# An attention, mixture-of-experts and gated FFN kernel: the parts of w_out made by the items of 512, w_in split in place, and groups that begin with the blocks still in SBUF

## The chip, the cores and the metric

The kernel runs on one core of one Trainium2 chip. The metric is the device time of one execution in microseconds (us). Before the change three runs took 1243.77 to 1248.26 us, median 1245.56. A separate, profiled execution took 1242.09 us, and its instructions span 1240.3 us; all durations in this document are from that execution.

The core has five engines with a queue each: TensorE (PE, matrix products; PEld are its weight loads), VectorE (DVE), ScalarE (ACT), GpSimd (POOL) and SyncE (SP, which here issues nearly all DMA requests).

## The reference, cut to what matters

Three stages follow one another: attention of 4096 rows against small states, a mixture of eight experts with one expert per token, and a gated FFN over 4608 tokens of width 512. The change touches the weights of the third stage, and the second stage only in that these weights are prepared beside it.

```python
# MoE: token t goes to one expert e
h = np.maximum(xc[mask] @ w1[e], 0.0)
y[mask] = gate_w[mask, None] * (h @ w2[e])
# FFN: w_in (512, 2048), w_out (2048, 512)
h = x @ w_in
relu6 = np.clip(h + 3.0, 0.0, 6.0)
g = h * relu6 / 6.0
return (g @ w_out).astype(np.float32)
```

## The kernel before, in words

**Number format.** The inputs are 64-bit floats. A float32 value is kept as two parts, hi (rounded to the shorter format `F32R` in which TensorE multiplies here) and lo (the rest), and a product is three matmuls: hi·hi, hi·lo, lo·hi (`PAIRS`). Making hi and lo is called a split: a copy on ScalarE (line 1239) and a subtraction on VectorE (line 1240).

**Stages.** Attention ends at about 130 us, with the routing of the tokens. The experts' tokens are then worked off in items of 512 (one written out in `first`, then a loop over `item_a`) until about 375 us, and in items of 128 (`item_b`) until about 449 us. The FFN takes the rest.

**Preparing w_in and w_out.** The 2048 hidden columns are 16 blocks f of 128. `Weights.load(f)` fetches a block's raw 64-bit w_in and w_out (512 KB each); `cut` makes float32 of them on VectorE with one step on ScalarE, four VectorE operations for each of the two; `keep` stores the float32 blocks (256 KB each) to a DRAM tensor `w32`. One block is cut during attention, three in the first item, and three in each round of the loop over `item_a`, at the places `LOAD_AT`, `CONV_AT` and `STORE_AT` of its eight steps. `again` fetches a block of `w32` back.

**FFN, first group.** 512 tokens (`first`) are multiplied plainly, block by block: `split_w(0, f)` and `split_w(1, f)` split the two weights into tiles W of [128, 2, 512], three buffers each; `stage_a(f)` makes h of the block in 12 matmuls (line 1308), applies the gate and splits g; `stage_b(f)`, two blocks later (`LAG`), adds the block's part of the output in 12 matmuls (line 1325). What is split is stored for the later groups: w_in's parts by `store_w`, four linear combinations of two blocks (made by `combine` from the float32 blocks, split, one pair p of blocks at a time) straight from a tile `both`, and w_out's parts by `store_o`. In DRAM, `wc` then holds 1792 KB for each of the eight pairs, and `wo` 1024 KB. In blocks 9, 11 and 13 `turn` also transposes and combines the x rows of the next group.

**FFN, groups of 768.** Five groups of 768 tokens use Strassen's scheme: `strassen(m)` computes seven products for one pair of blocks (line 1397), `second(m)` the output part (line 1449). Each of the 40 steps m reads back its pair of `wc` and `wo` (`load_c`, `load_o`), into two buffers each, two steps ahead; step m takes pair m mod 8.

**What sets the order.** The schedule is manual: each engine runs its instructions in the order in which the code is written, and waits at each for the data or buffers that it needs. SyncE's DMA requests are likewise in program order, so a request that waits holds those behind it. A request also waits until the eighth one before it, which had the same semaphore, has landed. The changed functions, with line numbers as in the profile:

## Time and profile before

| | |
|---|---|
| runs | 1243.77, 1245.56, 1248.26 us |
| profiled execution | 1242.09 us; span 1240.3 us |
| TensorE busy | 1160.9 us, 94% of the span |
| VectorE, ScalarE, GpSimd busy | 845.5, 503.0, 110.9 us |
| mean DMA rate | 221 GB/s, 273.68 MB in all |
| chain that ended last, by engine | PE 51%, DMA 6%, DVE 3%, ACT 2% |
| its largest lines | L1449 26%, L1397 23%, DMA `wc<-W` 4% |

A busy TensorE does not have to be at its peak: matmuls are pipelined, and the clock can be throttled to half. The granted clock is a share of full speed (2.4 GHz); a mean between 0.5 and 1 is a mix of the two levels. The chain of waits is followed back from the last instruction; a transfer in it, as `wc<-W`, is one for which an engine waited. A transfer is written destination<-source, by the names of tiles and DRAM tensors (`w` is `w32`; `cv`, `wf` and `W` are tiles in SBUF). In the lists of groups, `L1239` and `L1240` are the lines of the split helper and stand for many uses, which the tile names tell apart.

### The profile page before, as it was taken

How to read it: one execution, taken by the hardware profiler on the slowest of the kernel's cores; microseconds unless marked ns; L12 is line 12 of the kernel's file. 1: busy time of each engine (PE TensorE's matmuls, PEld its weight loads, DVE VectorE, ACT ScalarE, POOL GpSimd, SP SyncE). 2: the span in 40 equal slices, each digit the busy share in tenths (PEclk: the TensorE clock that was granted, in tenths of full speed). 3: DMA queues.
4: the chain of work that ended last, by engine and by line, in shares of the span. 5: the costliest groups of instructions: out<-in, count | busy, mean ns of one | idle time of the engine just before them, and what ended most of it. 6: DMA issues, size and time to landing. Idle time of an engine off the chain costs nothing.

```text
span 1240.3 us, 17749 instructions
## 1 busy us (share of the span) xinstructions
PE 1160.9 (94%) x6060; PEld 970.1 (78%) x6060; DVE 845.5 (68%) x1640; ACT 503.0 (41%) x955; POOL 110.9 (9%) x156
## 2 busy tenths in 40 slices
PE   7888999999998957778799999999999999999998
PEld 4665777888886635566699899889988999899997
DVE  6868787687681024456578876887688768876776
ACT  7776454354351123344243334333433343334331
POOL 4456301101101000000000000000000000000000
PEclk9889999999999978899999999999999999999999
DMA  6866887767666875666955565555655565456532
GB/s 191 269 220 204 295 263 254 235 222 254 241 216 231 298 273 180 249 227 233 368 200 198 204 229 213 203 191 212 218 196 202 203 238 186 173 187 238 185 144 85
DMA packets 103143, 273.68 MB, mean 221 GB/s; under 512 B 14240, under 2 KB 53152, under 8 KB 91040
## 3 DMA queue, kind: packets, MB, share of 16 engines
q1 hardware_dynamic: 98432, 261.20, 60.7%
q0 software_dynamic: 4640, 11.57, 2.6%
q8 instruction: 41, 0.67, 0.2%
q14 instruction: 30, 0.25, 0.1%
HBM read 208.47 MB, written 67.94 MB: 223 GB/s over the span
## 4 chain that ended last, share of the span: by engine, by line
PE 51%; DMA 6%; DVE 3%; ACT 2%; issue 1%; SPq 1%; ACTq 0%; DVEq 0%
PE o L1449 26%; PE b L1397 23%; DMA wc<-W 4%; DVE W L1240 1%; PE o L1235 1%; DMA wc<-wc 1%; ACT W L1239 1%; ACT both L1239 1%; PE b L1308 0%; DMA wo<-W 0%; DMA raw<-x_in_dram 0%; SPq L1178 0%; ACT g L1239 0%; SPq L1217 0%; DVE raw L1276 0%
## 5 line engine op out<-in xcount | busy, mean ns | idle before, releaser
L1449 PE MATMUL o<-wo,g 128*128 128x512 f32 x1440 | 334.3, 390 | 0.0
L1449 PEld LDWEIGHTS o<-wo,g 128*128 128x128 f32 x1440 | 269.7, 188 | 54.7
L1397 PE MATMUL b<-xc,wc 128*128 128x384 f32 x1680 | 301.2, 337 | 6.6 <-DMA wc<-wc 5.0
L1397 PEld LDWEIGHTS b<-xc,wc 128*128 128x128 f32 x1680 | 293.7, 189 | 9.3 <-issue 5.4
L1240 DVE TENSOR_TENSOR g<-cv,g 128x384 fp32r<-128x384 f32 x160 | 89.3, 558 | 92.8 <-ACT g L1239 92.8
L1239 ACT CAST g<-cv 128x384 fp32r<-128x384 f32 x160 | 82.2, 514 | 157.0 <-DVE cv L1251 157.0
L1458 DVE SCALAR_TENSOR_TENSOR W<-o,W 128x512 f32<-128x512 f32 x210 | 134.6, 681 | 3.5 <-PE o L1449 3.3
L872 PE MATMUL po<-w2p,hT 128*128 128x512 f32 x480 | 121.7, 401 | 0.0
L860 PE MATMUL ph<-xTa,w1p 128*128 128x512 f32 x480 | 117.4, 394 | 1.3 <-DVEq L1058 1.3
L1250 ACT ACTIVATE cv<-cv,three 128x384 f32<-128x384 f32 x80 | 49.3, 616 | 143.8 <-DVE cv L1411 136.3
L860 PEld LDWEIGHTS ph<-xTa,w1p 128*128 128x128 f32 x480 | 89.7, 188 | 22.8 <-issue 1.7
L872 PEld LDWEIGHTS po<-w2p,hT 128*128 128x128 f32 x480 | 89.9, 190 | 20.5 <-DVE hT L865 0.4
L1411 DVE TENSOR_TENSOR c<-b,c 128x384 f32<-128x384 f32 x160 | 87.0, 551 | 23.8 <-PE b L1397 23.2
L1308 PE MATMUL b<-xt,W 128*128 128x512 f32 x192 | 60.7, 472 | 26.1 <-ACT W L1239 25.4
L1308 PEld LDWEIGHTS b<-xt,W 128*128 128x128 f32 x192 | 43.4, 234 | 41.8 <-ACT W L1239 28.1
L1250 ACT ACTIVATE cv<-c,three 128x384 f32<-128x384 f32 x80 | 49.1, 614 | 15.0 <-DVE g L1240 15.0
L1411 DVE TENSOR_TENSOR cv<-b,cv 128x384 f32<-128x384 f32 x80 | 44.3, 554 | 14.3 <-PE b L1397 13.0
L1325 PE MATMUL o<-W,g 128*128 128x512 f32 x192 | 47.2, 393 | 2.9 <-ACT g L1239 2.9
L1251 DVE SCALAR_TENSOR_TENSOR cv<-cv,c 128x384 f32<-128x384 f32 x80 | 44.1, 552 | 5.8 <-ACT cv L1250 4.8
L277 PE MATMUL pxr<-BD,AT 128*128 128x265 f32 x128 | 42.2, 446 | 4.7 <-DVE AT L240 2.3
L775 DVE TENSOR_TENSOR w1p<-raw,w1p 128x512 fp32r<-128x512 f32 x48 | 31.9, 684 | 21.3 <-ACT w1p L774 16.6
L1325 PEld LDWEIGHTS o<-W,g 128*128 128x128 f32 x192 | 35.7, 188 | 12.1 <-ACT g L1239 3.7
(257 smaller groups left out, 1296.6 us busy)
## 6 DMA issues: line engine op xcount, KB each, us to landing
wc<-wc SPq DMA_DIRECT2D x40, 1792.0 KB, 7.1
raw<-in_moe_w_dram SPq DMA_DIRECT2D x80, 512.0 KB, 5.6
wo<-wo SPq DMA_DIRECT2D x40, 1024.0 KB, 6.0
raw<-in_moe_w_in_dram SPq DMA_DIRECT2D x16, 512.0 KB, 6.4
raw<-in_moe_w_out_dram SPq DMA_DIRECT2D x16, 512.0 KB, 5.0
x_in_dram<-XR SPq DMA_DIRECT2D x8, 1024.0 KB
w<-cv SPq DMA_DIRECT2D x32, 256.0 KB, 3.3
wc<-both SPq DMA_DIRECT2D x8, 1024.0 KB
```

What stands on the lines that cost most here:

```text
L860: nc.tensor.matmul(ph, lhsT=w1p[a][:, f, kk, :], rhs=xTa[b][:, kk, :], start=(n == 0), stop=(n == 11))
L872: nc.tensor.matmul(po[c], lhsT=hp[f][a][:, P * c:P * c + P], rhs=w2p[b][:, f, :], start=(f == 0 and n == 0), stop=(f == NF - 1 and n == 2),)
L1239: copy(hi, src)
L1240: nc.vector.tensor_tensor(lo, src, hi.bitcast(F32), op=ALU.subtract)
L1250: nc.scalar.activation(gg, h, AF.Relu, bias=k["three"])
L1251: nc.vector.scalar_tensor_tensor(gg, gg, 6.0, h, op0=ALU.min, op1=ALU.mult)
L1308: nc.tensor.matmul(ph, lhsT=W1[f][:, a, P * kk:P * kk + P], rhs=xt[b][:, kk, :], start=(n == 0), stop=(n == 11))
L1325: nc.tensor.matmul(pos[c], lhsT=gg[a][:, P * c:P * c + P], rhs=W2[f][:, b], start=(f == 0 and n == 0), stop=(f == NFF - 1 and n == 2),)
L1397: nc.tensor.matmul(t, lhsT=w[:, s:s + P], rhs=XC[m // NP][:, x, b, kk, :], start=(i == 0), stop=(i == 5))
L1411: v.tensor_tensor(c, t, u, op=ALU.add)
L1449: nc.tensor.matmul(po, lhsT=gs[f][a][:, o:o + P], rhs=w[:, DM * (2 * f + b):DM * (2 * f + b) + DM], start=(q == 0), stop=(q == 5),)
L1458: nc.vector.scalar_tensor_tensor(dst, po, 1.0 / 6.0, dst, op0=ALU.mult, op1=ALU.add)
```

## The change

- `cut` works on w_out first, then on w_in, and has a ninth step, `five`: it splits w_out's float32 block on ScalarE and VectorE into a tile `hl`. `keep` stores this pair of parts (512 KB) to `wo`, and w_in's float32 block (256 KB) to `w32`, now two tensors. `item_a` runs five steps instead of four in the second of each block's two places.
- The FFN no longer splits or stores w_out. It loads `wo` by pairs (`new_o`), two buffers, one pair ahead.
- w_in's parts and the combinations are written straight into one tile of 1792 KB per pair, in the layout of `wc` (two buffers of the pool that the groups use, and a third, `wcq`, for the pairs 2 and 5); `store(p)` stores it with one request. `stage_a` reads its weights there; the half of the odd block that the groups do not need is in a small tile `a21`.
- Each group of 768 starts with the two pairs that the stage before it ended with, which are still in SBUF; `pair_of` gives the order. Of 40 loads of each kind 30 are left in the groups.

```diff
--- before.py
+++ after.py
...
@@ -1001,7 +1001,7 @@
                     if f == CONV_AT[n]:
                         conv[n].begin()
                     if f in (CONV_AT[n], CONV_AT[n] + 1):
-                        conv[n].four()
+                        conv[n].some(4 + f - CONV_AT[n])
                 if f >= 1:
...
         self.raw = {}
 
         dram = tc.nc.dram_tensor
-        self.w32 = dram("w32", (NFF, 2, P, DM), F32, kind="Internal").ap()
+        self.w32 = dram("w32", (NFF, P, DM), F32, kind="Internal").ap()
+        self.wo = dram("wo", (NFF, P, 2 * DM), F32, kind="Internal").ap()
         self.wc = dram("wc", (NFF // 2, P, 7 * DM), F32, kind="Internal").ap()
-        self.wo = dram("wo", (NFF // 2, P, 4 * DM), F32, kind="Internal").ap()
 
...
-    def keep(self, f, a):
-
-        for i in range(2):
-            self.tc.nc.sync.dma_start(self.w32[ds(f, 1), i].rearrange("a p w -> p (a w)"), a[i])
-
-    def again(self, f, i, t=None):
-
-        t = self.room(i) if t is None else t
-        self.raw[f, i] = t
-        self.tc.nc.sync.dma_start(t, self.w32[f, i])
+            parts[i] = a[i]
+
+        def five():
+            t = parts[1] = self.two()
+            nc.scalar.copy(t[:, 0], a[1])
+            v.tensor_tensor(t[:, 1], a[1], t[:, 0].bitcast(F32), op=ALU.subtract)
+
+        return parts, [lambda g=g, i=i: g(i) for i in (1, 0) for g in (one, two, three, four)] + [five]
+
+    def keep(self, f, parts):
+
+        dma = self.tc.nc.sync.dma_start
+        dma(self.wo[ds(f, 1)].rearrange("a p w -> p (a w)"), parts[1].bitcast(F32).rearrange("p i w -> p (i w)"))
+        dma(self.w32[ds(f, 1)].rearrange("a p w -> p (a w)"), parts[0])
+
+    def again(self, f, t):
+
+        self.raw[f] = t
+        self.tc.nc.sync.dma_start(t, self.w32[f])
 
...
+    def load_w(f):
+        if f < NFF:
+            W.again(f, qp.tile([P, DM], F32, tag="wf", name="wf", bufs=4))
+
+    def new_c():
+        return sp.tile([P, 7 * DM], F32R, tag="wc", name="wc")
+
+    def new_o(p):
+        t = sp.tile([P, 4 * DM], F32R, tag="wo", name="wo")
+        nc.sync.dma_start(
+            t.bitcast(F32).rearrange("p (f w) -> p f w", f=2), W.wo[2 * p:2 * p + 2].rearrange("f p w -> p f w")
+        )
         return t
 
-    def split_w(i, f):
-        t = new_w(i, f)
-        split(t[:, 0], t[:, 1], W.raw[f, i])
+    def split_w(f):
+        p, odd = divmod(f, 2)
+        if not odd:
+            t = wc[p] = qp.tile([P, 7 * DM], F32R, name="wcq") if p % 3 == 2 else new_c()
+            split(t[:, 0:DM], t[:, DM:2 * DM], W.raw[f])
+        else:
+            a21[p] = qp.tile([P, 2, 2 * P], F32R, tag="a21", name="a21", bufs=2)
+            t = wc[p][:, 2 * DM:3 * DM].rearrange("p (i f) -> p i f", i=2)
+            for to, u in ((a21[p], 0), (t, 2 * P)):
+                split(to[:, 0], to[:, 1], W.raw[f][:, u:u + 2 * P])
 
     def combine(p):
 
-        a1, a2 = ([W.raw[2 * p + i, 0][:, 2 * P * u:2 * P * u + 2 * P] for u in range(2)] for i in range(2))
+        a1, a2 = ([W.raw[2 * p + i][:, 2 * P * u:2 * P * u + 2 * P] for u in range(2)] for i in range(2))
         t = W.scratch(1).bitcast(F32)
         s = [t[:, 2 * P * i:2 * P * i + 2 * P] for i in range(4)]
...
-        nc.sync.dma_start(W.wc[p, :, 3 * DM:].rearrange("p (i f) -> p i f", i=2), both.bitcast(F32))
-
-    def store_w(f):
-        p, o = divmod(f, 2)
-        if o == 0:
...
+    def store(p):
+        nc.sync.dma_start(W.wc[p], wc[p].bitcast(F32))
+
+    def w1(f, a, kk):
+        p, odd = divmod(f, 2)
+        if odd and kk < 2:
+            return a21[p][:, a, P * kk:P * kk + P]
+        o = 2 * DM + 2 * P * a + P * (kk - 2) if odd else DM * a + P * kk
+        return wc[p][:, o:o + P]
 
...
@@ -1368,17 +1389,27 @@
         return rest
 
 
-    wc, wo = {}, {}
+    pair_of, pos_of = [], list(range(NP - 2, NP)) + list(range(NP - 2))
+    for n in range(len(groups)):
+        pair_of += pos_of
+        pos_of = pos_of[-2:] + pos_of[:-2]
+    cm, om = {}, {}
 
     def load_c(m):
-        if m < NP * len(groups):
-            wc[m] = sp.tile([P, 7 * DM], F32R, tag="wc", name="wc")
-            nc.sync.dma_start(wc[m].bitcast(F32), W.wc[m % NP])
+        if m < total:
+            p = pair_of[m]
+            if m < 2:
+                cm[m] = wc[p]
+            elif m % NP < 2:
+                cm[m] = cm[m - 2]
+            else:
+                cm[m] = new_c()
+                nc.sync.dma_start(cm[m].bitcast(F32), W.wc[p])
 
     def load_o(m):
-        if m < NP * len(groups):
-            wo[m] = sp.tile([P, 4 * DM], F32R, tag="wo", name="wo")
-            nc.sync.dma_start(wo[m].bitcast(F32), W.wo[m % NP])
+        if m < total:
+            p = pair_of[m]
+            om[m] = wo[p] if m < 2 else om[m - 2] if m % NP < 2 else new_o(p)
 
 
...
@@ -1474,19 +1505,19 @@
             fetch(pairs.pop(0))
 
 
+    for p in range(2):
+        wo[p] = new_o(p)
+    load_w(2)
+    load_w(3)
     fetch(32, True)
     fetch(0, True)
     for f in range(2):
-        split_w(0, f)
-    load_w(0, 2)
-    load_w(0, 3)
-    split_w(1, 0)
+        split_w(f)
     combine(0)
     todo = []
     for c, (c0, h) in enumerate(first):
         pt = transposed(out_bank(), xw[c0][:, h])
         split(xt[0][:, :, P * c:P * c + P], xt[1][:, :, P * c:P * c + P], pt)
-    load_w(1, 2)
     fetch_next()
     fetch_next()
     new_xc(0, cp)
@@ -1494,33 +1525,31 @@
     LAG = 2
     for f in range(NFF + LAG):
         if f < NFF:
+            load_w(f + 4)
+            if f % 2 == 0:
+                store(f // 2)
             stage_a(f)
             if f + 2 < NFF:
-                load_w(0, f + 4)
-                split_w(0, f + 2)
+                split_w(f + 2)
                 if f % 2:
                     combine((f + 2) // 2)
-            if f + 1 < NFF:
-                split_w(1, f + 1)
-                load_w(1, f + 3)
         if f >= LAG:
             stage_b(f - LAG)
-        if f < NFF:
-            store_w(f)
-            store_o(f)
+            if f % 2 and f // 2 + 1 < NP:
+                wo[f // 2 + 1] = new_o(f // 2 + 1)
         for low in todo:
             low()
         todo = []
         if f in turns:
             todo.append(turn(0, turns[f], [bank(2), bank(3)]))
             fetch_next()
-        if f >= NFF - 2:
-            load_c(f - NFF + 2) if f < NFF else load_o(f - NFF)
+    for m in range(2):
+        load_c(m)
+        load_o(m)
     out_first()
     q0.close()
     cp1 = ctx.enter_context(tc.tile_pool(name="f_c1", bufs=1))
     turns = {1: 0, 3: 1, 5: 2}
-    total = NP * len(groups)
     for m in range(total + 1):
         n, p = divmod(m, NP)
```

**Order, SyncE, where the FFN begins.** These are the first requests after the loop of the items of 128, before the change. `raw` is the tile of x rows, `wf` and `cv` hold float32 blocks of w_in and w_out; the waits in brackets are semaphores, DMAHW0 to 7 those of the earlier requests.

```order
L1217 DMA raw_3002<-x_in_dram 32x512 [waits DMASW5_49,DMASW4_49,DMAHW4_49,DMASW3_49,DMASW2_49]
L1217 DMA raw_3002<-x_in_dram 32x512 [waits DMAHW5_49]
L1217 DMA raw_3002<-x_in_dram 32x512 [waits DMAHW6_49]
L1217 DMA raw_3002<-x_in_dram 32x512 [waits DMAHW7_49]
L1217 DMA raw_3002<-x_in_dram 32x512 [waits DMAHW0_49]
```

And after it, at the same place, where `wo` is the pair tile of w_out's parts:

```order
L1286 DMA wo<-wo 128x2x1024 [waits DMAHW2_49,DMASW5_49,DMAHW4_49,DMASW4_49,DMAHW5_49,DMASW3_49,DMAHW6_49,DMASW2_49,DMAHW7_49,Activation_49,Pool_49]
L1286 DMA wo<-wo 128x2x1024
L1189 DMA wf<-w 128x512 x2
L1228 DMA raw_3027<-x_in_dram 32x512 x2
L1228 DMA raw_3027<-x_in_dram 32x512 [waits DMAHW0_49]
L1228 DMA raw_3027<-x_in_dram 32x512 [waits DMAHW1_49]
L1228 DMA raw_3027<-x_in_dram 32x512 [waits DMAHW2_49]
L1228 DMA raw_3027<-x_in_dram 32x512 [waits DMAHW3_49]
L1228 DMA raw_3027<-x_in_dram 32x512 [waits DMAHW4_49]
L1228 DMA raw_3027<-x_in_dram 32x512 [waits DMAHW5_49]
```

Two pairs of `wo` and two blocks of w_in now stand ahead of the x rows, and the fifth to eighth x request waits for the semaphores of just these four.

**Order, SyncE, one pair of blocks in the first group.** Before, for one even and one odd block (`both` are the combinations, `W` the split weights, `128x2x256` the odd block's half):

```order
L1178 DMA wf<-w 128x512
L1279 DMA wc<-both 128x2048
L1178 DMA cv_3140<-w 128x512
L1286 DMA wc<-W_3017 128x2x256
L1292 DMA wo<-W_3096 128x1024
L1178 DMA wf<-w 128x512
L1178 DMA cv_3172<-w 128x512
L1284 DMA wc<-W_3093 128x1024
L1292 DMA wo<-W_3137 128x1024
```

After, two pairs:

```order
L1315 DMA wc<-wc 128x3584
L1189 DMA wf<-w 128x512
L1286 DMA wo<-wo 128x2x1024
L1189 DMA wf<-w 128x512
L1315 DMA wc<-wcq 128x3584
L1189 DMA wf<-w 128x512
L1286 DMA wo<-wo 128x2x1024
L1189 DMA wf<-w 128x512
```

Nine requests per pair, five of them stores, have become four, one of them a store.

**Order, VectorE, in an item of 512.** Before, from one block's second conversion to the next step's ReLU part (`hT`), w_out's float32 block is `cv_2583`:

```order
L1161 SCALAR_TENSOR_TENSOR cv_2583<-raw_2485,cv_2583 128x512
L1165 ISA
L1165 SCALAR_TENSOR_TENSOR cv_2583<-raw_2485,cv_2583 128x512
L775 REGISTER_ALU
L775 TENSOR_TENSOR w1p_1858<-raw_0_96,w1p_1857 128x512
```

And after, where this place works on w_in (`cv_2595`) and then subtracts for w_out's parts (`hl`):

```order
L1165 SCALAR_TENSOR_TENSOR cv_2595<-raw_2496,cv_2595 128x512
L1169 ISA
L1169 SCALAR_TENSOR_TENSOR cv_2595<-raw_2496,cv_2595 128x512
L1176 REGISTER_ALU
L1176 TENSOR_TENSOR hl<-cv_2557,hl 128x512
L775 REGISTER_ALU
L775 TENSOR_TENSOR w1p_1861<-raw_0_96,w1p_1860 128x512
```

One subtraction has come in ahead of the item's own split of its expert weights (`w1p`).

## Rows read from the trace of the kernel before

**Rows 1.** Table by stage: microseconds, busy time (instructions) of each engine, clock, DMA
```profile
130.00:184.00 54.00, 51.07 (x251) 41.27 (x250) 44.65 (x117) 24.96 (x48) 11.08 (x11) 0.97 0.83 284
285.00:335.00 50.00, 50.00 (x226) 40.60 (x225) 36.79 (x62) 22.37 (x41) 8.07 (x12) 1.00 0.72 241
449.00:459.30 10.30, 3.91 (x17) 3.17 (x17) 6.69 (x12) 5.05 (x8) 0.00 (x0) 0.50 0.70 230
513.00:531.00 18.00, 13.76 (x53) 10.59 (x51) 8.59 (x14) 6.52 (x11) 0.00 (x0) 0.91 0.60 220
585.00:600.00 15.00, 7.18 (x27) 4.46 (x26) 7.19 (x12) 4.49 (x7) 0.00 (x0) 1.00 1.02 364
600.00:615.00 15.00, 13.41 (x68) 13.09 (x68) 8.02 (x16) 5.08 (x10) 0.00 (x0) 0.89 1.03 392
754.00:1219.80 465.80, 465.80 (x2372) 421.32 (x2371) 352.65 (x661) 171.77 (x320) 0.00 (x0) 1.00 0.55 197
```

**Rows 2.** Chain of waits: start, length (us), what held it, in the first group
```profile
459.29 5.04 PE b L1308 x12
...
487.69 3.82 DMA wc<-W
...
497.75 4.85 DMA wc<-W
...
504.96 3.88 DMA wc<-W
```

**Rows 3.** Groups by form, 459.3 to 585: count, busy us, mean ns, idle before, releasers
```profile
L1308 PE MATMUL b<-xt,W 128*128 128x512 f32 x192 | 60.7, 472 | 26.1 <-ACT W L1239 25.4 <-issue 0.7
...
L1250 ACT ACTIVATE gg<-b,three 128x512 f32<-128x512 f32 x15 | 10.3, 685 | 5.2 <-PE b L1308 5.2
L1240 DVE TENSOR_TENSOR g<-gg,g 128x512 fp32r<-128x512 f32 x14 | 9.7, 692 | 9.6 <-ACT g L1239 9.6
...
L1240 DVE TENSOR_TENSOR W<-cv,W 128x512 fp32r<-128x512 f32 x14 | 9.6, 683 | 0.0
L1251 DVE SCALAR_TENSOR_TENSOR gg<-gg,b 128x512 f32<-128x512 f32 x14 | 9.5, 679 | 5.2 <-ACT gg L1250 5.2
L1239 ACT CAST g<-gg 128x512 fp32r<-128x512 f32 x14 | 8.7, 620 | 17.7 <-DVE gg L1251 17.7
...
L1240 DVE TENSOR_TENSOR both<-raw,both 128x1024 fp32r<-128x1024 f32 x7 | 8.6, 1225 | 7.8 <-ACT both L1239 7.8
L1239 ACT CAST both<-raw 128x1024 fp32r<-128x1024 f32 x7 | 7.4, 1051 | 15.6 <-DVE raw L1276 15.6
L1235 PE MATMUL b<-ident,raw 128*128 128x128 f32 x24 | 3.1, 272 | 0.0
L1276 DVE TENSOR_TENSOR raw<-wf,raw 128x256 f32<-128x256 f32 x7 | 3.0, 425 | 0.2
```

**Rows 4.** Timeline where the first group of 768 begins
```profile
599.76 13.24 PE L1397 MATMUL b<-xc,wc 128*128 128x384 f32 x66 [4.96 <-DMA wc<-wc]
```

**Rows 5.** Timeline inside an item of 512, TensorE
```profile
242.15 2.94 PE L860 MATMUL ph<-xTa,w1p 128*128 128x512 f32 x12
...
247.72 2.94 PE L860 MATMUL ph<-xTa,w1p 128*128 128x512 f32 x12
```

**Rows 6.** DMA issues, whole kernel: size of each, median us to landing
```profile
wc<-wc SPq DMA_DIRECT2D x40, 1792.0 KB, 7.1
...
wo<-wo SPq DMA_DIRECT2D x40, 1024.0 KB, 6.0
...
cv<-w SPq DMA_DIRECT2D x18, 256.0 KB, 3.7
...
wf<-w SPq DMA_DIRECT2D x14, 256.0 KB, 5.0
...
wc<-W SPq DMA_DIRECT2D x8, 256.0 KB, 7.6
```

**Rows 7.** SyncE's own waits, whole kernel: us in total, times, longest
```profile
SPq L1172 <- DMA w<-cv: 53.2, 12, 5.6
```

More of the change, by code (lines that the diff above doesn't have):

```diff
@@ L969, in begin, with some @@
                 c.a, c.steps = self.W.cut(c.raw)
-            def four(c):
-                for step in c.steps[:4]:
+            def some(c, n):
+                for step in c.steps[:n]:
                     step()
-                del c.steps[:4]
+                del c.steps[:n]
             def store(c):
@@ L1061, in run @@
         for f in range(2):
-            for i in range(2):
-                self.W.again(f, i)
+            self.W.again(f, self.W.room(0))
         turned32(xb[:, 0:DM], x32)
@@ L1125, in room, with two @@
         return self.rp.tile([P, DM], F32, tag=f"cv{i}", name=f"cv{i}", bufs=2)
+    def two(self):
+        return self.rp.tile([P, 2, DM], F32R, tag="hl", name="hl", bufs=3)
     def load(self, f):
@@ L1143, in cut @@
         a, m = [None, None], [None, None]
+        parts = [None, None]
         words = [r.rearrange("p (f w) -> p f w", w=2) for r in raw]
@@ L1165, in four @@
             v.scalar_tensor_tensor(a[i], m[i], least, a[i], op0=ALU.is_ge, op1=ALU.mult)
-        return a, [lambda g=g, i=i: g(i) for i in range(2) for g in (one, two, three, four)]
-    def keep(self, f, a):
-        for i in range(2):
-            self.tc.nc.sync.dma_start(self.w32[ds(f, 1), i].rearrange("a p w -> p (a w)"), a[i])
-    def again(self, f, i, t=None):
-        t = self.room(i) if t is None else t
-        self.raw[f, i] = t
-        self.tc.nc.sync.dma_start(t, self.w32[f, i])
+            parts[i] = a[i]
[11 more added lines that the diff above has]
+        self.tc.nc.sync.dma_start(t, self.w32[f])
 def ffn(tc, ctx, W, x_in, out, k):
@@ L1254, in halves @@
         return [t[:, i] for i in range(2)]
-    W1, W2 = {}, {}
-    def new_w(i, f):
-        (W1, W2)[i][f] = t = sp.tile([P, 2, DM], F32R, tag=f"W{i}", name=f"W{i}", bufs=3)
-        return t
-    def split_w(i, f):
-        t = new_w(i, f)
-        split(t[:, 0], t[:, 1], W.raw[f, i])
+    wc, wo, a21 = {}, {}, {}
+    total = NP * len(groups)
+    first = [(32, 0), (32, 1), (0, 0), (0, 1)]
+    q0 = ExitStack()
+    qp = q0.enter_context(tc.tile_pool(name="f_q", bufs=1))
+    xt = [qp.tile([P, 4, 512], F32R, name=f"xt{i}") for i in range(2)]
+    def load_w(f):
[8 more added lines that the diff above has]
+        )
+        return t
+    def split_w(f):
[8 more added lines that the diff above has]
+                split(to[:, 0], to[:, 1], W.raw[f][:, u:u + 2 * P])
     def combine(p):
-        a1, a2 = ([W.raw[2 * p + i, 0][:, 2 * P * u:2 * P * u + 2 * P] for u in range(2)] for i in range(2))
+        a1, a2 = ([W.raw[2 * p + i][:, 2 * P * u:2 * P * u + 2 * P] for u in range(2)] for i in range(2))
         t = W.scratch(1).bitcast(F32)
@@ L1276, in combine @@
         v.tensor_tensor(s[3], a1[1], s[1], op=ALU.subtract)
[L1277 to L1301 removed]
+        split(wc[p][:, 3 * DM:5 * DM], wc[p][:, 5 * DM:], t)
+    def store(p):
[6 more added lines that the diff above has]
+        return wc[p][:, o:o + P]
     def stage_a(f):
@@ L1308, in stage_a @@
                 nc.tensor.matmul(
-                    ph, lhsT=W1[f][:, a, P * kk:P * kk + P], rhs=xt[b][:, kk, :], start=(n == 0), stop=(n == 11)
+                    ph, lhsT=w1(f, a, kk), rhs=xt[b][:, kk, :], start=(n == 0), stop=(n == 11)
                 )
                 n += 1
-        gg = qp.tile([P, 512], F32, tag="gg", name="gg")
+        gg = W.room(1)
         gate(ph, gg)
@@ L1325, in stage_b @@
                 nc.tensor.matmul(
-                    pos[c], lhsT=gg[a][:, P * c:P * c + P], rhs=W2[f][:, b], start=(f == 0 and n == 0),
+                    pos[c], lhsT=gg[a][:, P * c:P * c + P], rhs=wo[f // 2][:, DM * (f % 2 * 2 + b):][:, 0:DM], start=(f == 0 and n == 0),
                     stop=(f == NFF - 1 and n == 2),
@@ L1332, in out_first @@
             c0 = first[2 * u][0]
-            oc = new_w(u, "out").bitcast(F32)
+            oc = W.two().bitcast(F32)
             nc.scalar.mul(oc[:, 0], pos[2 * u], 1.0 / 6.0)
@@ L1438, in second @@
         gs = [g.pop((m, i)) for i in range(2)]
-        w = wo.pop(m)
+        w = om[m]
         for c in range(6):
@@ L1442, in second @@
             if p == 0 and h == 0:
-                acc[i] = new_w(n % 2, ("out", n, i)).bitcast(F32)
+                acc[i] = W.two().bitcast(F32)
             po = out_bank()
@@ L1610, in begin @@
                 todo.extend(steps + [lambda: W.keep(f, a)])
-            return [begin] + [lambda: todo.pop(0)() for _ in range(9)]
+            return [begin] + [lambda: todo.pop(0)() for _ in range(10)]
         todo = []
```

19 lines of the change are left out of this document (1 added, 18 removed).

## The prediction

> **What bounds the kernel now.** I read the table by stage first [rows 1]. From 754 to 1219.8 us TensorE is busy 465.80 of 465.80 at a granted clock of 1.00: the groups of 768 tokens are TensorE's, and fewer loads there buy nothing. The items of 512 (285 to 335) are the same: TensorE 50.00 of 50.00, VectorE 36.79, ScalarE 22.37. The exception is the FFN's first group, about 459 to 600: in 513 to 531 TensorE is busy 13.76 of 18 us at clock 0.91, VectorE 8.59, ScalarE 6.52, DMA share 0.60. Nothing is full there, so something goes round in a circle.
>
> The chain of waits [rows 2] shows it: "DMA wc<-W" returns at every block, and from 487.69 to 504.96, one pair of blocks, takes 17.27 us. A tile of W is made, stored, and made again only when its store three blocks earlier has landed; SyncE's queue, nine requests per pair, holds the next store behind the combinations. The table by form [rows 3] agrees: TensorE's `stage_a` matmuls sat idle 26.1 us, 25.4 for ScalarE's W. At the end [rows 4] TensorE waits 4.96 us more, until 599.76, for `wc` to be read back.
>
> How much of this is needed? In the items one block of 24 such matmuls goes from 242.15 to 247.72 [rows 5]: 5.57 us, 0.232 us each. The group has 16 blocks: 89.1 us, where the trace has 459.29 to 594.80 (599.76 less the 4.96) = 135.5.
>
> **The first group after the change.** Removed: 16 splits of w_out (one 0.62 us copy on ScalarE and one 0.683 us subtraction on VectorE each [rows 3]), the 16 stores of 512 KB behind them, the store-before-reuse circle of W, the four read-backs (2 x 1792 and 2 x 1024 KB) at the end. Added: eight loads of 1024 KB of `wo`. The w_in parts are made in place, in three pair tiles in turn, and each pair is one store of 1792 KB, issued about four blocks before its tile is reused: about 22 us for something that lands in 7 when read [rows 6].
>
> *Start.* SyncE leaves the loop at the same moment, but puts 2 x 1024 KB of `wo` and 2 x 256 KB of w_in ahead of the x rows that `stage_a` needs, and four of the last six x requests also wait for those to land. A 256 KB request stuck behind others shows what a queue costs: the `wc<-W` stores of 256 KB land in 7.6 us, loads of 256 KB into `cv` in 3.7 [rows 6]. 2.62 MB at the 392 GB/s of 600 to 615 [rows 1] is 6.7 us. Bounds: 0 if the x rows pass the others, 22 if the four land one after another (6.0 + 6.0 + 5.0 + 5.0 [rows 6]). I take 6.7, nearest to the rate row: first `stage_a` matmul at 459.29 + 6.7 = 466.0.
>
> The Trainium skill, page "DMA: Bandwidth & Descriptors", section "Queues, rings and completion order", says that each DMA engine consumes a queue's descriptors in ring order. The 7.6 against 3.7 agrees with it. By that rule the sum carries the whole 6.7; without it the start would not move and the forecast would be 6.7 lower.
>
> *Length.* Matmuls 89.1; the 24 transposes of the three turns 3.1 [rows 3]; the first twelve matmuls at half clock (5.04 [rows 2] instead of 12 x 0.232 = 2.8) 2.3; a gap of 0.6 before the third block, whose split follows the first block's gate. Beside this run ScalarE and VectorE, now with less to do. Their chain per pair, by durations of [rows 3]: even block: ReLU 0.685, times h 0.679, cast 0.62, subtraction 0.692, split of w_in 0.683 = 3.4. Odd block: the same 2.7 to the gate's end, two half-width subtractions 0.8, four combinations of 0.425 = 1.7, cast 1.051, subtraction 1.225 = 7.4. Together 10.8 against TensorE's 11.1: covered, since `stage_b` lags two blocks, but just. A pair with a turn adds five half-width operations and two subtractions on VectorE (5 x 0.42 + 0.69 + 1.22 = 4.0) and 1.0 on TensorE: 14.8 against 12.2, so up to 2.6 shows per such pair; the lag absorbs part; I take 1.2 each, 3.6. Sum 98.7 (bounds 95.1 without turns' excess, 112 with it in full and the clock below). End at 564.7.
>
> Transfers as cover: per pair 1.84 MB stored, 1.05 + 0.52 loaded, 3.4 MB, which at 364 GB/s (585 to 600 [rows 1]) is 9.4 us of 11.1. So TensorE is next, with ScalarE/VectorE and DMA both within two microseconds of it.
>
> *Clock.* Granted clock is 0.50 (1.2 GHz) in 449 to 459.3 after the wait for the last scatter, 0.91 in the holed stretch, 1.00 where TensorE never stops [rows 1]. I assume 1.00 after the first block. The skill's page "TensorE: Matmul & The Clock Gate", section "HAM oscillation", says that idle gaps between bursts send the array back to half rate. The rows agree in direction. If gaps remain and 0.91 stays, 92.2 us of TensorE work takes 101: 9 more.
>
> *Into the groups.* The blocks of the first two steps are in SBUF, so the 4.96 us wait goes; that is part of the difference of the ends, 599.76 - 564.7 = 35.1. From there to the steady state ScalarE and VectorE pace both kernels (13.41 of 15 TensorE at 0.89 in 600 to 615 [rows 1]); I leave it at 0. The ten pairs of loads saved later lie under a full TensorE: 0.
>
> **What moves into the items.** 16 copies and 16 subtractions, the same forms. Twelve come in the loop: 3 x 0.683 more on VectorE per item, 36.79 to 38.8 of 50, 22.37 to 24.2 on ScalarE. TensorE covers that unless a block is locally full: between 0 and 12 x 0.683 = 8.2; I take 0.5. The stores grow by 256 KB each, but the second of the two no longer waits for the first (now different tensors; SyncE waited 53.2 us in 12 such waits [rows 7]), so what is queued behind it, the next loads, starts earlier; nothing on TensorE waits for these, so no gain. Three come in the first item (130 to 184), where VectorE is busy 44.65 of 54 and TensorE already waits 2.9 us: 0 to 2.1, I take 1.5. One falls to the attention: 0 to 0.7, I take 0.5. Together 2.5 (0 to 11).
>
> **Sum.** Profiled execution 1242.09 (span 1240.3 and 1.8 around it) - 35.1 + 2.5 = 1209.5. The median shown, 1245.56, lies 3.5 above that execution; half of this goes on top: 1211. Its own range, from the bounds that I think likely together (start 4 to 10, length 96 to 104, items 0 to 6): 1203 to 1221.
>
> **Rivals.**
> *Transfers pace the group.* For: DMA runs at 220 GB/s today in this stretch with a share of only 0.6 [rows 1], so latency may be what limits it, and store, load and x rows share one queue. 8 x 3.4 MB less the first two `wo` loads is 25.1 MB, at 220 GB/s 114 us: end at 580, gain 19.8, time 1227. Against: buffers are two to four deep and 364 to 392 GB/s are shown at the end of this same stage. 18%.
> *The items pay in full.* VectorE is locally full in blocks with a conversion (2.5 us of conversion, 0.68 more, three more of about 0.69, of 5.57): all 11 appear, 1220. Against: 13 us of slack per item. 6%.
> *The change doesn't overlap what it says:* `stage_a` waits for each gate-and-split chain and each chain for `stage_a`: 2 x 2.8 + 10.8 = 16.4 per pair, 131 in all, end at 597: time 1244 against 1245.56, no change. Against: order and lag above. 4%.
> *The round trip gets longer (slower).* SyncE still waits at each 1792 KB store for that pair's last subtraction, and loads are queued behind it. If load, split, combination, store and the next `wo` load then follow one another, a pair takes 5.0 + 7.5 + 7.1 + 6.0 = 25.6 us, 205 in all, time about 1318. It decides once a pair takes more than about 16.4 us, (599.76 - 466.0 - 2.5) / 8. Against: w_in is loaded four blocks ahead. 4%.
>
> **How the numbers follow.** Forecast 68%, then 18, 6, 4 and 4. The range 1197 to 1233 holds the forecast's own range, the items' case and the transfers' case, and below 1203 a start that does not move. About 0.3% (4 us) is what a measurement of this kernel can tell from no change. Faster 0.92, same 0.04, slower 0.04.
>
> **What would show it.** In the profile after: first `stage_a` matmul near 466 plus the items' 2.5; `stage_a` without idle time for ScalarE's cast; about 5.6 us per block; first matmul of the first group of 768 near 567, with no "DMA wc" before it; the items' slices unchanged on TensorE; DMA near 300 GB/s in the first group; from there to the end the same 640 us. Wrong if: blocks take 7 us or more with "DMA wo" or "DMA wf" as releaser (transfers); TensorE waits in the items for VectorE's hT or po; x rows land later than 10 us after the loop's end.

## The result, and the profile after

The changed kernel takes 1203.53 us (median of 4 runs, 1201.31 to 1206.39), the kernel before, run beside it, 1246.2 us: a ratio of 0.966, 95% interval 0.963 to 0.969. The profiled execution took 1204.09 us; its span fell from 1240.3 to 1202.3, by 38.0.

The table by stage for the kernel after, with the columns of [rows 1] (length; busy time and instructions of TensorE, its weight loads, VectorE, ScalarE, GpSimd; granted clock; DMA share; GB/s). Its stages are: an item of 512, the gap between the items and the FFN, the part of the first group that holds most of the turns' work, the begin of the groups of 768, and the long middle of the groups.

```profile
285.00:335.00 50.00, 50.00 (x226) 40.61 (x225) 38.43 (x63) 24.26 (x44) 8.82 (x14) 1.00 0.78 256
450.00:466.60 16.60, 3.65 (x16) 3.27 (x16) 6.11 (x12) 4.62 (x8) 0.00 (x0) 0.50 0.74 243
...
523.00:553.00 30.00, 30.00 (x142) 24.98 (x141) 23.73 (x46) 16.25 (x30) 0.00 (x0) 1.00 0.70 266
...
563.00:578.00 15.00, 13.40 (x78) 13.04 (x77) 9.79 (x19) 5.27 (x11) 0.00 (x0) 1.00 0.58 193
718.00:1183.80 465.80, 465.80 (x2368) 420.84 (x2367) 352.95 (x662) 171.05 (x317) 0.00 (x0) 1.00 0.44 159
```

In the item TensorE still has no free moment while VectorE went from 36.79 to 38.43 us. In the first group, where TensorE had been busy 13.76 of 18 us, it is now busy 30.00 of 30. In the groups the DMA share fell from 0.55 to 0.44 and 465.80 us of TensorE stayed 465.80.

The chain of waits of the kernel after (start, length, what held it) where [rows 2] had "DMA wc<-W" at every block:

```profile
451.85 7.13 DMA wf<-w
459.00 3.04 DMA raw<-x_in_dram
462.29 3.65 PE o L1246 x16
...
466.65 5.52 PE b L1329 x12
...
478.19 2.72 PE o L1346 x12
480.91 2.72 PE b L1329 x12
```

Blocks now follow one another at 2 x 2.72 us, and the wait for W's stores is gone. New at the top is a wait for W_in ahead of the x rows. The groups by form of the same stretch, 466.6 to 563.1, answer to [rows 3]: TensorE's idle time before `stage_a` was 26.1 us, and is 0.8 + 0.0 + 1.3.

```profile
L1346 PE MATMUL o<-wo,g 128*128 128x512 f32 x192 | 47.0, 392 | 0.7 <-ACT g L1250 0.7
...
L1329 PE MATMUL b<-xt,wc 128*128 128x512 f32 x108 | 29.6, 420 | 0.8 <-issue 0.7
...
L1329 PE MATMUL b<-xt,a 128*128 128x512 f32 x48 | 12.2, 389 | 0.0
...
L1329 PE MATMUL b<-xt,wcq 128*128 128x512 f32 x36 | 9.2, 396 | 1.3 <-DVE wcq L1251 1.3
```

And the timeline where the first group of 768 begins, answering to [rows 4], has no wait in brackets:

```profile
563.08 11.63 PE L1428 MATMUL b<-xc,wc 128*128 128x384 f32 x66
```

With four moments read off the timelines of every run (first matmul of the items; SyncE's first request of the FFN, "exit"; first `stage_a` matmul; first Strassen matmul), the span divides as follows, in us. The names are those of the experiments below.

| kernel | first item to exit | exit to stage_a | stage_a to Strassen | Strassen to end | span |
|---|---|---|---|---|---|
| before | 316.1 | 10.4 | 140.5 | 640.5 | 1240.3 |
| after | 317.7 | 15.7 | 96.4 | 639.2 | 1202.3 |
| e1 reload | 318.7 | 15.9 | 97.2 | 639.1 | 1202.8 |
| e2 x first | 318.7 | 10.5 | 96.6 | 639.3 | 1197.8 |
| e3 w_out in the FFN | 319.2 | 14.1 | 101.8 | 639.2 | 1205.8 |
| e4 deep (before) | 315.1 | 10.5 | 104.5 | 641.4 | 1205.0 |
| e5 five twice | 332.9 | 15.6 | 91.0 | 639.2 | 1202.1 |
| e6 two stores | 319.3 | 15.6 | 92.0 | 639.3 | 1189.8 |
| e8 two tiles | 318.9 | 16.1 | 91.1 | 639.2 | 1191.0 |
| e9 early store (before) | 317.9 | 10.5 | 105.2 | 641.0 | 1199.4 |
| e10 after again | 319.2 | 15.8 | 94.1 | 639.2 | 1199.2 |
| e11 x first, two tiles | 317.9 | 10.1 | 92.4 | 639.3 | 1189.6 |
| e7 x first, turns | 320.4 | 10.4 | 93.0 | 639.2 | 1195.6 |

The whole gain is in the third column. What precedes the first item varies from set to set with the same code (131 to 134 us in before, after and e1 to e4, 123 to 126 in e5 to e9, 130 to 133 in e10, e11 and e7), and the kernel before had medians of 1246.0, 1238.4 and 1243.1 beside these sets. So times are compared as ratios to the kernel before of the same set, spans only by columns.

### The profile page after: what moved, and what is told of

It reads as the page before. It is cut to its first block, busy times and chain, and to the rows that moved or that the text cites. A ratio compares the mean times of both kernels' runs of the same rounds, so it can differ in the third digit from the quotient of the medians.

```text
span 1202.3 us, 17646 instructions
## 1 busy us (share of the span) xinstructions
PE 1146.1 (95%) x6060; PEld 962.2 (80%) x6060; DVE 845.6 (70%) x1648; ACT 502.9 (42%) x963; POOL 110.4 (9%) x156
## 2 busy tenths in 40 slices
DMA packets 98342, 244.84 MB, mean 204 GB/s; under 512 B 13280, under 2 KB 50144, under 8 KB 92640
## 4 chain that ended last, share of the span: by engine, by line
PE 56%; DVE 3%; DMA 1%; ACT 1%; issue 1%; SPq 0%; DVEq 0%; ACTq 0%
PE o L1480 27%; PE b L1428 24%; PE b L1329 2%; PE o L1346 1%; PE o L1246 1%; ACT g L1250 1%; DVE cv L1262 1%; DMA wf<-w 1%; DVE wc L1251 1%; DMA wc<-wc 1%; ACT wc L1250 0%; DVE xc L1388 0%; DMA raw<-x_in_dram 0%; DVE g L1251 0%; DVE xc L1387 0%
## 5 line engine op out<-in xcount | busy, mean ns | idle before, releaser
L1480 PE MATMUL o<-wo,g 128*128 128x512 f32 x1440 | 334.3, 390 | 0.0
L1480 PEld LDWEIGHTS o<-wo,g 128*128 128x128 f32 x1440 | 269.7, 188 | 54.7
L1251 DVE TENSOR_TENSOR g<-cv,g 128x384 fp32r<-128x384 f32 (+1 forms) x176 | 100.4, 571 | 103.8 <-ACT g L1250 103.8
L1250 ACT CAST g<-cv 128x384 fp32r<-128x384 f32 (+1 forms) x176 | 92.1, 523 | 181.6 <-DVE cv L1262 181.6
L1489 DVE SCALAR_TENSOR_TENSOR hl<-o,hl 128x512 f32<-128x512 f32 x210 | 134.7, 682 | 3.5 <-PE o L1480 3.3
L1346 PE MATMUL o<-wo,g 128*128 128x512 f32 x192 | 47.0, 392 | 0.7 <-ACT g L1250 0.7
L1262 DVE SCALAR_TENSOR_TENSOR cv<-cv,cv 128x384 f32<-128x384 f32 x80 | 43.9, 549 | 0.0
L1346 PEld LDWEIGHTS o<-wo,g 128*128 128x128 f32 x192 | 35.7, 188 | 9.7 <-ACT g L1250 1.5
L1452 ACT COPY c<-b 128x384 f32<-128x384 f32 x40 | 19.2, 480 | 55.1 <-PE b L1428 54.9
L1164 ACT ACTIVATE raw<-raw 128x512 f32<-128x512 f32 x32 | 22.1, 690 | 46.2 <-DVE cv L1160 46.0
```

The lines of the kernel that those rows point to most:

```text
L1250: copy(hi, src)
L1251: nc.vector.tensor_tensor(lo, src, hi.bitcast(F32), op=ALU.subtract)
L1262: nc.vector.scalar_tensor_tensor(gg, gg, 6.0, h, op0=ALU.min, op1=ALU.mult)
L1346: nc.tensor.matmul(pos[c], lhsT=gg[a][:, P * c:P * c + P], rhs=wo[f // 2][:, DM * (f % 2 * 2 + b):][:, 0:DM], start=(f == 0 and n == 0), s ...
L1480: nc.tensor.matmul(po, lhsT=gs[f][a][:, o:o + P], rhs=w[:, DM * (2 * f + b):DM * (2 * f + b) + DM], start=(q == 0), stop=(q == 5),)
L1489: nc.vector.scalar_tensor_tensor(dst, po, 1.0 / 6.0, dst, op0=ALU.mult, op1=ALU.add)
```

## The experiments

**What paid: the circle.** e4 is the kernel before with one edit, the tiles of W_in four deep instead of three; w_out, the separate pair tiles and all loads stay as they were.

```
-  ... tag=f"W{i}", name=f"W{i}", bufs=3)
+  ... tag=f"W{i}", name=f"W{i}", bufs=4 - i)
```

> The kernel before, with the w_in tiles W four deep instead of three (more does not fit beside its other tiles). Nothing else is changed: the same stores, loads, splits and queue. Theory A1 (the circle split, store, reuse holds the first group): a split may now wait for a store one block older, the 40.5 us that ScalarE waits for DMA wc<-W mostly go, and a pair falls from 17.3 us to what ScalarE and VectorE or the queue need, 13.5 to 15: 18 to 30 us less, 1216 to 1228. Theory A3 (SyncE's queue itself, nine requests per pair in order, each waiting for the combinations or for the eighth request before it, is what holds): less than 5 us, 1241 or more.

Measured: 1208.26 us, 0.970 (0.967 to 0.973). The idle time of ScalarE before its copy into a W_in tile, by form, first in the kernel before (459 to 600), then in e4 (459 to 585):

```profile
L1239 ACT CAST W<-wf 128x512 fp32r<-128x512 f32 x14 | 8.7, 619 | 40.5 <-DMA wc<-W 40.5
```
```profile
L1239 ACT CAST W<-wf 128x512 fp32r<-128x512 f32 x14 | 8.6, 618 | 2.7 <-DMA wc<-W 2.7
```

One more buffer gives 35.3 of the 38.0 us of span, more than the 18 to 30 us of A1, whose mechanism it shows; A3 falls. Is it memory, then, that the kernel before lacked? e9 goes back to three tiles and only issues each store one block earlier.

```
+    store_w(0)
     for f in range(NFF + LAG):
...
-            store_w(f)
+            if f + 1 < NFF:
+                store_w(f + 1)
```

> Tests the circle in the kernel before without giving it a byte more of SBUF. The kernel before with its three tiles of W_in, in which the store of a tile is issued one block earlier: that of tile 0 ahead of the loop, that of tile f+1 at the end of block f. Theory A (the store was issued so late that its landing fell into the time in which the tile was wanted again): the wait of ScalarE for W's stores, 40.5 us in the kernel before, falls below 10 us and the time comes to that of the kernel before with four tiles, 1206 to 1212. Theory B (three tiles are too few, whenever the store is issued): the wait stays above 25 us and the time above 1230.

Measured: 1201.12 us, 0.9685 (0.9636 to 0.9735), which is 1207 us at the 1246 us that the kernel before took in the first set: theory A, with not a byte more. By form, ScalarE's same row and TensorE's `stage_a` in e9, 453 to 570:

```profile
L1239 ACT CAST W<-wf 128x512 fp32r<-128x512 f32 x14 | 8.6, 617 | 5.8 <-DMA wc<-W 5.8
```
```profile
L1308 PE MATMUL b<-xt,W 128*128 128x512 f32 x192 | 49.5, 405 | 3.2 <-ACT W L1239 2.2 <-issue 0.7
```

The tile was finished long before its store was issued; the store, at the end of the block that read the tile, had one block (5.6 us) to land before the tile was wanted, and an odd block's store takes 7.6 [rows 6]. Given two blocks it fits. e8 asks the same of the kernel after: the third pair tile is taken away.

```
-  t = wc[p] = qp.tile([P, 7 * DM], F32R, name="wcq") if p % 3 == 2 else new_c()
+  t = wc[p] = new_c()
```

> Tests what the third tile of a pair (the single buffer named wcq) is worth. The kernel after without it: the eight pairs go through two tiles in turn, so that a tile is made anew two blocks (10.9 us) after the store of what it held was issued. Theory A (what matters is that the store is issued long enough ahead of the next use; it lands 7 us after its issue, inside 10.9): at most 2 us longer, below 1206. Theory B (the number of tiles is what matters, and with two the circle of make, store and make again is back): the wait for the store stands ahead of the blocks again, and the kernel is 10 to 20 us longer, 1214 to 1224.

Measured: 1191.98 us, 0.962 (0.957 to 0.967); theory B falls. TensorE's `stage_a` in e8, by form, 460.7 to 551.7, waits for no store:

```profile
L1329 PE MATMUL b<-xt,wc 128*128 128x512 f32 x144 | 36.4, 395 | 1.1 <-issue 0.7 <-DVE xt L1251 0.3
```

**The loads that are saved.** e1 is the kernel after, but all eight pairs of every group, the two still in SBUF too, are read back from DRAM (40 loads of each kind instead of 30), in the old order m mod 8.

```
-            p = pair_of[m]
...
+            cm[m] = new_c()
+            nc.sync.dma_start(cm[m].bitcast(F32), W.wc[m % NP])
...
+            om[m] = new_o(m % NP)
```

> The changed kernel, but every group of 768 reads back all eight pairs of wc and wo (40 loads of each kind instead of 30, and the first two pairs are read back where the first group ends). Theory A (the gain comes from the first group, where TensorE no longer waits for the store-before-reuse circle): from the second step on nothing changes under a full TensorE; only the wait for the read-back returns, 5 us before the change and here 3 to 8, so about 1208.5 us, with the wait in the trace between the last output matmul of the first group and the first Strassen matmul. Theory B (the saved 28.8 MB of loads are what pays): more than half of the 42.7 us is lost, 1225 us or more, spread over the five groups.

Measured: 1202.93 us, 0.966 (0.963 to 0.968), no different from after. Its timeline where the first group begins has a wait of 1.07 us, far below the expectation of theory A; theory B falls too:

```profile
563.69 2.51 PE L1421 MATMUL b<-xc,wc 128*128 128x384 f32 x13 [1.07 <-DMA wc<-wc]
```

Neither beginning with blocks in SBUF nor 28.8 MB of traffic (273.67 MB in e1, 244.84 in the kernel after) is worth anything that the time shows.

**Where w_out is split.** e3 puts the split of w_out back into the FFN: the items store its float32, the FFN loads, splits and stores it, and keeps the rest of the kernel after.

```
-  return parts, [ ... ] + [five]
+  return parts, [ ... ]
...
+            split_o(f)
+            load_wo(f + 3)
+            if f % 2:
+                store_o(f // 2)
```

> The changed kernel, but w_out is split in the first group of the FFN again: the items store its float32 block, the first group loads it, splits it into the pair tile wo and stores that, with one store per pair. Theory A1 (what pays is that the tiles are deep enough, so that no split waits for a store; the work itself nearly fits): the chain of ScalarE and VectorE per pair grows by 2 x 1.3 from 10.8 to 13.4 us against 11.1 of TensorE, so 8 x 2.3 = 18 us more, about 1222 us, DMA above 300 GB/s. Theory A2 (moving w_out's split away is what pays): most of the 42.7 us is lost, 1235 us or more, with TensorE waiting as before. The items' share of about 0.5 us comes back in either.

Measured: 1209.55 us, 0.972 (0.969 to 0.976): the direction of A1 at a third of its size; A2 falls. In e3, by form, 464.7 to 566.6, the second half of a block waits for w_out:

```profile
L1366 PE MATMUL o<-wo,g 128*128 128x512 f32 x192 | 49.1, 402 | 5.5 <-ACT wo L1251 3.4 <-DVE wo L1252 2.1
```

e5 prices the same work where the change put it: every copy and subtraction of `five` is done twice.

```
-  nc.scalar.copy(t[:, 0], a[1])
-  v.tensor_tensor(t[:, 1], a[1], t[:, 0].bitcast(F32), op=ALU.subtract)
+  for _ in range(2):
+      nc.scalar.copy(t[:, 0], a[1])
+      v.tensor_tensor(t[:, 1], a[1], t[:, 0].bitcast(F32), op=ALU.subtract)
```

> Prices the split of w_out's items. The kernel after, with the copy on ScalarE and the subtraction on VectorE of every split of an item's result done twice. Theory A (inside the loop of the items these two instructions lie beside other work): the period from one item's first matmul to the next stays at 46.31 us, only the first item, which nothing overlaps, grows by 0.4 to 0.8 us, and the last item ends less than 1.5 us later. Theory B (the items pay for the split, hidden by something else that got faster): each item's period grows by 1 us or more, and the last item ends 4 us or more later.

Measured by its one profile: theory A falls. The items take 332.9 us against 318.9 to 319.3 of the kernels with the same items in its set; from the last transposes of one item to those of the next, 229.84 to 279.89, are 50.05 us where the kernel after has 46.30. TensorE is no longer full (table by stage, 285 to 335, then TensorE's waits from 130 to 376: us in total, times, longest):

```profile
285.00:335.00 50.00, 47.67 (x207) 38.27 (x206) 37.75 (x64) 24.24 (x44) 5.44 (x8) 0.97 0.73 244
```
```profile
PE ptx L781 <- DVE xTa L775: 7.5, 5, 1.9
PE ph L860 <- ACT w1p L774: 3.8, 2, 2.3
PE ptx L781 <- DMA xn<-xs_dram: 3.3, 3, 1.5
```

Three more splits per item, 3 x (0.61 + 0.69) = 3.9 us, cost 3.75 us in this item; in the four items of the loop it is 4.3, 3.75, 3.8 and 1.2. The first set of splits was free in the loop; the second, as e5 has it, is paid for about in full in three items of four.

But e5 does more than add work. The second copy writes where the first subtraction still reads, so ScalarE waits for VectorE (15.7 us in the 16 doubled splits) and then VectorE for ScalarE (11.0 us): one of them takes VectorE from 251.88 to 253.95, three times its 0.69. A second set of splits that don't wait for each other was not run and may cost less. What e5 shows is that VectorE's 11.6 us of idle time in 50 (285 to 335 of the kernel after) do not take in such a chain; where blocks are converted VectorE has no pause to give (10.84 us busy of the 11.19 from 249.83 to 261.02 in the kernel after).

**The start.** e2 requests the x rows ahead of `wo` and W_in.

```
+    fetch(32, True)
+    fetch(0, True)
+    load_w(2)
+    load_w(3)
     for p in range(2):
         wo[p] = new_o(p)
-    load_w(2)
...
```

> The changed kernel, with the requests for the x rows of the first group put ahead of the two wo pairs and the two w_in blocks. Theory A (the x rows wait behind 2.6 MB in the same queue): the first matmul of the first group comes 10.4 us after the loop's end as before the change, not 15.7, and the time falls by about 5.4 us to 1198, if wo and w_in are then still in time for the second and third block; if w_in comes too late for the third block's split, half of it is given back (1200.5). Rival (the start is late for another reason, such as the splits ahead of it on ScalarE and VectorE): no change, 1203.5.

Measured: 1200.35 us, 0.965 (0.962 to 0.968). SyncE's requests from the exit on, in the kernel after and then in e2 (start, us, requests), and TensorE's first work in e2:

```profile
450.92 0.89 SPq L1286 DMA_DIRECT2D wo<-wo  x2
451.85 1.07 SPq L1189 DMA_DIRECT2D wf<-w  x2
452.96 8.23 SPq L1228 DMA_DIRECT2D raw<-x_in_dram  x10
```
```profile
451.43 4.54 SPq L1228 DMA_DIRECT2D raw<-x_in_dram  x10
456.09 0.83 SPq L1189 DMA_DIRECT2D wf<-w  x2
457.03 0.89 SPq L1286 DMA_DIRECT2D wo<-wo  x2
```
```profile
456.13 1.94 PE L1246 MATMUL o<-ident,raw 128*128 128x128 f32 x8 [10.53 <-DMA raw<-x_in_dram]
...
461.92 5.74 PE L1329 MATMUL b<-xt,wc 128*128 128x512 f32 x12 [0.72 <-issue]
```

The ten requests take 8.23 us behind the others and 4.54 ahead of them, and `stage_a` begins 10.5 us after the exit, as it did before the change. By this moment it is theory A; the time, 1200.35, is that of its half case, and its interval overlaps that of the kernel after.

**The long store.** e6 tries a stretch of 6.1 us without work on VectorE (last section): the store of a pair in two requests.

```
-  nc.sync.dma_start(W.wc[p], wc[p].bitcast(F32))
+  o, n = ((0, 3 * DM), (3 * DM, 4 * DM))[i]
+  nc.sync.dma_start(W.wc[p, :, o:o + n], wc[p][:, o:o + n].bitcast(F32))
```

> Tests the 6.1 us stretch in which VectorE stands still without a wait while a store of 1792 KB fills the DMA engines. The kernel after, with the store of a pair issued as two requests, the first 768 KB at the even block and the other 1024 KB at the odd one, 5.4 us later. Theory A (VectorE's next instructions are fetched behind the store, and a shorter store holds them up for less): the idle stretch falls from 6.1 to 3 us or less, and the kernel gets 1 to 3 us shorter, about 1201 to 1202. Theory B (the stretch has nothing to do with the size of the store): it stays at 5 to 6 us, and the time within 0.1% of the kernel after.

Measured: 1192.12 us, 0.9625 (0.959 to 0.966): the stretch of 6.1 is now one of 4.44, one instruction earlier (507.69), which is neither theory's figure; and e5, whose FFN is the unchanged one, had no such stretch in this set, and its stage was as short (91.0 against 92.0). So e6 alone decides nothing. Hence a second run of the kernel after.

> The kernel after, unchanged, run again, so that the two kernels below have it beside them on the same chip, and to learn what of the differences between the first two sets of runs is the kernel's. In the runs of five_twice, whose FFN is that of the kernel after, the stretch from the first stage_a matmul to the first Strassen matmul took 91.0 us, where the kernel after had 96.4. Theory A (these 5.4 us belong to the run: the clock granted at the start of the stretch, 0.88 of full against 1.00, and the 6.1 us in which VectorE stood still): in this run too both are absent or both there whatever the kernel, and the ratio to the kernel before stays between 0.963 and 0.969. Theory B (they belong to the kernels): 96 us with the idle stretch of VectorE again.

Measured: 1203.17 us, 0.968 (0.9645 to 0.971). Both theories are half right. TensorE's first `stage_a` work and the begin of the groups in e10, and VectorE's row:

```profile
465.89 0.47 PE L1329 MATMUL b<-xt,wc 128*128 128x512 f32 x1 [0.72 <-issue]
466.56 2.79 PE L1329 MATMUL b<-xt,wc 128*128 128x512 f32 x11 [0.21 <-DVE xt L1251]
...
560.01 10.24 PE L1428 MATMUL b<-xc,wc 128*128 128x384 f32 x58
```
```profile
517.80 0.69 DVE L1251 TENSOR_TENSOR wcq<-wf,wcq 128x512 fp32r<-128x512 f32 x1 [5.85 <-issue]
```

The slow first block is the run's: 12 matmuls in 5.52 us in after, in 3.5 here. The idle stretch is the program's: 5.85 us at the same instruction. It is worth more than the wait of 1.0 to 1.3 us that TensorE has just behind it. `stage_b`'s row above, 47.0 us busy and 0.7 of waiting, is the same in e10, e1 and e2 to 0.1. In e8, which has no such stretch, it reads:

```profile
L1346 PE MATMUL o<-wo,g 128*128 128x512 f32 x192 | 45.8, 389 | 0.0
```

It is the same in e5, e7 and e11. With the `wcq` tile (9.2 us and 1.0 of waiting in e10, 8.9 and none in e5) that is 3.2 us: all of the 94.1 against 91.0 of e5. e6, with its shorter stretch, lies between (46.4 and 0.4).

**Early rows with two tiles, and the turns.** e11 joins e2 and e8; e7 is e2 with the turns spread over the blocks.

> Two of the edits that looked best, together: the kernel after with the rows of x requested ahead of w_out and W_in at the start of the FFN, and with two tiles of a pair instead of three. Theory A (the early rows are worth their 4.5 us, the third tile nothing): 4 to 5 us below the kernel after run beside it, its first stage_a matmul 10.5 us after the last request of the items and not 15.7. Theory B (the gain of the earlier rows was scatter): within 1.5 us of the kernel after.

Measured: 1194.17 us, 0.9607 (0.9576 to 0.9638), below the interval of e10 beside it: 9 us less in medians, 9.6 in span, of which 5.7 at the start and 1.7 in the stage; 1.0 lies ahead of the items and 1.3 in them, where no edit is. That is theory A at twice its size. The 1.7 are the idle stretch, which e11 lacks (3.2), less a slower first block (4.89 against 3.46). Its first `stage_a` work and the begin of its groups:

```profile
457.90 4.89 PE L1329 MATMUL b<-xt,wc 128*128 128x512 f32 x12 [0.72 <-issue]
...
550.31 11.63 PE L1428 MATMUL b<-xc,wc 128*128 128x384 f32 x66
```

```
-    turns = {9: 0, 11: 1, 13: 2}
+    turns = {3: 0, 8: 1, 13: 2}
```

> Tests what paces the three pairs of blocks that hold a turn (the transposes and splits of the next column of x), 12.5 us a pair against 10.9. The kernel after with the early rows of x, and the three turns moved from blocks 9, 11 and 13 to 3, 8 and 13. Theory A (TensorE itself: it was busy for 30.0 of the 30.0 us from 523 to 553, and a turn's transposes cost it the same anywhere): the stretch keeps its length within 0.5 us, the time that of the kernel above within 0.2%. Theory B (the chain of ScalarE and VectorE, which spread turns would relieve, as the prediction has it): 1 to 2.5 us less.

Measured: 1197.15 us, 0.961 (0.957 to 0.9645), like e11; its stage is 93.0 us against 92.4. The first blocks (5.46 and 4.89) make up these 0.6, and after its first block TensorE waits nowhere in the stage. Spreading the turns gives nothing against e11: theory A, TensorE is what is full there. (e2, with the turns where they were, took 96.6 in another set, with VectorE's full idle stretch; in e7 1.50 us of it are left.) e7 also keeps the third tile, which again makes no difference that can be measured.

## Why the prediction was right, step by step

*The circle* was the right mechanism, and e4 and e9 show it to be nearly the only one: of the 44.1 us by which the stage of the first group became shorter, 36.0 come with one more tile alone (140.5 to 104.5) and 35.3 with the moment of the store alone (to 105.2), the wait of 4.9 us at the end still in both. The prediction did not see that most of the gain could be had by issuing one store a block earlier. The Trainium skill, page "Perfetto Trace Analysis", section "Optimization Strategy", says that a gap that repeats on the engine that should be full can mean too little SBUF for the next tile. e4 agrees. e9 shows the same gap closed at the old number of tiles: TensorE's idle time before `stage_a` went from 26.1 us [rows 3] to 3.2, ScalarE's wait from 40.5 to 5.8.

*The start*: 6.7 us forecast, 5.4 measured (10.4 to 15.7). That the order of the requests does it is shown by e2 and e11, which give all of it back. Of the prediction's two ways the trace shows the waits: in the kernel after SyncE stands 3.2 us until the two `wo` have landed and 1.0 until the two `wf` have, before it can issue the fifth to eighth x request. These waits and the 2.0 us of the four requests ahead are enough for the 5.4. The ring order that the prediction weighed (the Trainium skill, page "DMA: Bandwidth & Descriptors", section "Queues, rings and completion order") is not told apart from them by any run, and the 7.6 against 3.7 in which the prediction saw it compares stores with loads. One sign of being wrong came true: x rows were to land within 10 us of the loop's end, and the ones that TensorE waited for landed 11.1 us after it (459.00 + 3.04 - 450.92). The sign was set against the prediction's own sum, which adds 6.7 to the 7.6 of before.

*The length*: 98.7 forecast, 96.4 and 94.1 measured. Mis-sized are the matmuls, 16 x 5.44 = 87.0 instead of the 89.1 taken from the items' row, and the turns' excess of 3.6 us. The chain of ScalarE and VectorE does not show in the pairs with a turn: from one block's second half to that two blocks on, 529.47 to 541.26, are 11.8 us, TensorE's own 10.9 and 0.8 for the transposes. Not in the sum were 1.7 us at the wcq tile and 1.9 at the end, where the last three second halves, waiting for gates, take 10.0 us instead of 8.2; of the kernels with after's FFN only those with VectorE's idle stretch have both. So that 98.7 lay so near is partly luck: terms 5.7 us too large stand against 3.6 that it did not have. Its 2.3 us for a first block at the low clock were there in after (5.52 us for 12 matmuls instead of 2.72) and mostly not in e10.

*The end*: wait of 4.96 us gone, as forecast. That the loads saved in the groups are worth 0 is shown by e1, and the last column, 639.1 to 639.3 in all kernels with after's groups against 640.5, leaves 1.3 us for all the rest.

*The items*: 2.5 us forecast. From first item to exit the kernels with after's items took 317.7 to 320.4, those with before's 315.1 to 317.9: 2.5 between the means, 318.9 of eight (e3, e5 left out) and 316.4 of three. The loop's share is 0, against 0.5 forecast: its period is 46.3 us in before and after. About 2.2 of the 2.5 lie in the first item: from its first matmul to its last transposes are 48.5 to 50.7 us with before's items and 50.9 to 52.8 with after's. But e3, without `five`, takes 51.2 there and 319.2 in all. So the split that the prediction priced is not shown to be the reason, the agreement of 2.5 with 2.5 is luck as far as these runs go, and the cause stays open.

*The sum*: 1211 forecast, 1203.53 measured; 1209.5 for the profiled execution, 1204.09 measured. The gain of 42.7 between the medians also holds what the prediction halved, since this time the timed runs did not lie above the profile.

*The rivals*: "transfers pace the group" fell at once (220 to 266 GB/s, no wait for `wo` or `wf` in the blocks), and so did the longer round trip; from one second half to that two blocks on are 10.9 to 13.4 us. "The items pay in full" did not come either. Its premise holds, as VectorE is full where a block is converted, and e5 shows what a longer chain there costs.

And the rest of the edit? Against e9 and e4, which keep w_out in the FFN and read everything back, the kernel after has 8 to 11 us less in the stage and 1.8 to 2.2 in the groups, but 5 more at the start and 2.5 in the items; the ratios (0.966 and 0.968 against 0.9685 and 0.970) cannot be told apart. The order of the first requests (5) and the idle stretch (3) hide its worth in part: e11, without either, lies below e4 (0.964 at most against 0.967 at least), while its interval still touches that of e9; both were run in other sets.

## What to carry to other kernels

Where a buffer is stored and then reused, count the time from the issue of the store to the next write, not the buffers: issuing the store when the data is ready gave 39 (33 to 45) of 42 us by the ratios, with no memory. Loads requested ahead of a phase's first ones delay that phase (here 2.6 MB by 5 us), so request first what the first instruction needs. And look where an engine's idle time lies before calling it slack: VectorE, idle for 12 us of 50, took three splits per item for nothing, but three more, chained to the first, cost about their full length in three items of four. Doubling a piece of work tests this only if the copy doesn't wait for the original.
